# Sixteen consecutive tokens per partition, and V kept on chip with a shifted copy

## The chip, the cores and the metric

The kernel runs on one core of a Trainium2 chip. The metric is the device time of one execution in microseconds; lower is better. The core's engines work side by side, each through its own list of instructions in a fixed order: TensorE (PE, with PEld for its weight loads), VectorE (DVE), ScalarE (ACT), GpSimd (POOL) and SyncE (SP), which here only issues DMAs. DMAs are also issued from ACT and POOL. Sixteen DMA engines carry them all.

## The reference

2048 tokens of width 512 are normalised, and three terms are added: the input, a sliding dilated attention, and a gated MLP that mixes tokens.

```python
x = A_x                                   # (1, 2048, 512)
xn = layernorm(x)
# A: 32 heads of 16; each token looks at 8 tokens: itself and 2, 4, ... 14 before it
qkv = xn @ wqkv
idx = pos[:, None] - 2 * arange(8)[None, :]          # masked where negative
logits = einsum('bhsd,bhswd->bhsw', q, k[idx]) * 16 ** -0.5
o = einsum('bhsw,bhswd->bhsd', softmax(logits), v[idx])
A = o.reshape(B, S, D) @ wo
# B: gated MLP, hidden width 2 * 896
z = gelu(xn @ w_in)
z1 = z[..., :896]
z2 = layernorm(z[..., 896:])
g = einsum('ts,bsf->btf', w_sp, z2) + b_sp[None, :, None]     # w_sp is 2048 x 2048
B_ = einsum('bsf,fd->bsd', z1 * g, w_out)
return x + A + B_
```

## The kernel before

All tensors on chip lie in one bf16 array, `arena`, in which regions are reused as they fall free; fp32 scalars lie in `fpool`. Python code adds tasks (`T`, `dma`) with what they read and write; a planner derives the waits from these and from overlaps of the ranges, and the order of each engine's tasks is written out by hand in `plan.orders`, one list for each of PE, ACT, DVE, POOL and SP. An engine works through its list strictly in that order. Two tasks whose ranges overlap, one of them writing, are ordered as the program adds them.

Tokens come in 16 blocks of 128, in four groups j of 512. The first part of the program runs group by group:

- `ln_block(b)`: statistics of a block of x on DVE (L647, L650), the inverse root on POOL (L652), the normalisation on DVE (L662), then a transpose into `xnT`, on PE for the first four blocks and by DMA (L666) for the others.
- `qk_pair(j, c)`: Q and K of a group (L733), with heads interleaved so that four chunks c hold them, and one eviction by ACT for both (L741). The last 16 columns of K are copied by POOL into the next group's pad (L747). Q and K have two buffers each, by j % 2.
- `v_block(b)`: V of 128 tokens (L713), evicted by ACT (L717) and written to a scratch tensor in DRAM, `vscr`, by POOL's DMAs (L720).
- `prod_reduce(j)`: DVE multiplies Q with eight shifted views of K, 128x4096 (`prod`, L757). Of the four chunks' products some are summed on DVE (`psum`, L762), chosen by `npadd`, and PE sums over the dimensions and what is left (`stream`, L772, tasks `lg`). ACT evicts the logits (L794) and a DMA transposes them (L798, tasks `pT`).
- `softmax(j)`: on DVE and ACT for each group when its logits are there (L809 to L846; the exp at L826).
- `z2_block`, `z2_sq`, `z2_wave(j)`: the second half of the MLP's input with GELU (L856, L862), its squares (L913), mean and variance for four blocks (L921 to L931), the inverse root on POOL (L934) and the normalisation on DVE (L937), then sums of blocks T1 to T4 for the gate (L954).
- `z1_block(b)`: the first half (L900, L907).

The second part runs over eight tiles t, each of two times 128 tokens. `ld_w` transposes the rows of `w_sp` of a tile by two DMAs (L963, tasks `w`, two slots by t % 2); `s_sums` adds blocks of them on DVE (L975 to L981); `gate_parts` makes the gate by seven products of eight matmuls each (L1017, tasks P1 to P7), a Strassen-like scheme in which ACT copies partial results (L1032, L1035) and DVE finishes (L1059, L1063); `u_op` multiplies by z1 on DVE (L1041) and transposes by DMA (L1043, `uT`). `pv_pair` reloads nine shifted rows of V for 128 partitions from `vscr` (L1144, 1152 KB a pair), multiplies by the attention weights (L1152), sums (L1156, L1160) and transposes by DMA (L1165, `OTd`). `out_block` loads the residual (L1184), puts it into PSUM by ACT (L1191), adds the two output products (L1196 with `wo`, L1200 with `w_out`), evicts (L1209) and stores (L1212). `w_out` is loaded at L1128 and `wo` at L1131, whose DRAM side is `[[512, 4], [16*512, 32], [4*512, 4], [1, 512]]`.

In this program a partition holds every fourth token of 512: `tok(b)` gives the first token and the step 4 for z1, the gate, V and the output.

Of the kernel before, what the change touches and what calls it, by code (L numbers as in the profile page):

```python
# [14 lines left out]
class Plan:  # L15
# [288 lines left out]
BF = mybir.dt.bfloat16  # L304
F16 = mybir.dt.float16
F32 = mybir.dt.float32
ALU = mybir.AluOpType
# [11 lines left out]
    npadd=((1, 2), (1, 2, 3), (1, 2, 3), (1, 2, 3)),  # L319
# [5 lines left out]
def build_kernel(nc, A_x, A_wqkv, A_wo, B_x, B_w_in, B_w_sp, B_b_sp, B_w_out, out, report=False, sched_kw=None,  # L325
# [17 lines left out]
    VR = 8 + S // 2  # L343
    vscr = nc.dram_tensor("vscr", (2 * VR, 512), BF).ap()

    def tok(b):
        return (512 * (b // 4) + b % 4, 4)

    def rows(ap2, b):
        t0, ts = tok(b)  # L350
        w = ap2.shape[1]
        return bass.AP(tensor=ap2.tensor, offset=ap2.offset + t0 * w, ap=[[ts * w, 128], [1, w]])
# [3 lines left out]
    NT = 8  # L356
    off = {}
    base = 0
    for k, v in dict(xin=0, xn=2048, wqk=4096, wv_raw=8192, xin2=10240, Vn=12288).items():
        off[k] = base + v  # L360
    off["W"] = base
    base += 16384
    off["OT"] = base
    off["xnT"] = base
    base += 4 * S
    off["w_in"] = base
    off["w_out"] = base
    off["wo"] = base + FC * 512
    base += 7168
    off["QT"] = base  # L370
    off["KT"] = base + 4 * 512 * NQ
    ksz = 2 * 4 * (512 + KP)
    off["Vs"] = off["QT"]
    base = off["KT"] + ksz
    off["pb"] = base
    off["L"] = base + 8192
    off["Ve"] = base + 9728
    off["On"] = base + 4608
    off["yout"] = base + 6656
    off["xres"] = base + 8192  # L380
    veo = (0, -9728)
    base += 14336
# [8 lines left out]
    off["maskt"] = base + FH  # L391
# [3 lines left out]
    off["zeros"] = base  # L395
    off["Za"] = base
    base += 512
    for name, n in (("R", 128), ("ident", 128), ("mx", 128), ("Zb", 256), ("hm", 32), ("bsb", 16)):
        off[name] = base
        base += n  # L400
        base = (base + 15) & ~15
# [4 lines left out]
    for name, n in (("prime", 4), ("Z", 128), ("st6", NB * 9),  # L406
                    ("mv", NB * 2), ("vpe", NB), ("rstd", NB), ("s1", 2 * NB), ("s2", NB), ("m2", NB), ("msq", NB),
                    ("vpe2", NB), ("rstd2", NB), ("mhalf", 4), ("bias", NB), ("P5s", 2 * HF)):
        foff[name] = fb
        fb += n  # L410
# [4 lines left out]
    with ExitStack() as es:  # L415
# [36 lines left out]
        def k_off(c, j):  # L452
            return off["KT"] + (4 * (j % 2) + c) * (512 + KP) + KP

        for c in range(4):
            for j in range(NJ):
                R(("KTpad", c, j), "sb", [(k_off(c, j) - KP, k_off(c, j))])
                R(("QT", c, j), "sb", [(q_off(c, j), q_off(c, j) + 512)])
                R(("KT", c, j), "sb", [(k_off(c, j), k_off(c, j) + 512)])
        for s_ in range(NPB):  # L460
            R1(("pb", s_), "pb", 4096, 4096 * s_)
        for s_ in range(2):
            R1(("On", s_), "On", 1024, 1024 * s_)
            R1(("Vs", s_), "Vs", 4096, 4096 * s_)
            R1(("Ve", s_), "Ve", 4608, veo[s_])
            for r_ in range(2):
                R1(("w", s_, r_), "W", 2048, 8192 * s_ + 2048 * r_)
                R1(("g", s_, r_, 0), "g", HF, FH * (2 * s_ + r_))
                R1(("g", s_, r_, 1), "g", HF, FH * (2 * s_ + r_) + HF)
            for r_ in range(4):  # L470
                R1(("S", s_, r_), "W", 1024, 8192 * s_ + 4096 + 1024 * r_)
            R(("P5s", s_), "f", [(foff["P5s"] + HF * s_, foff["P5s"] + HF * s_ + HF)])
        for s_ in range(4):
# [3 lines left out]
            R1(("Vn", s_), "Vn", 512, 512 * s_)  # L477
        for s_ in range(3):
            R1(("xres", s_), "xres", 512, 512 * s_)
            for q in range(8):  # L480
                R1(("yout", s_, q), "yout", 64, 512 * s_ + 64 * q)
# [14 lines left out]
        for b in range(NB):  # L496
            R(("xnT", b), "sb", [(off["xnT"] + dc * S + 128 * b, off["xnT"] + dc * S + 128 * b + 128)
                                 for dc in range(4)])
            R1(("OT", b), "OT", 512, 512 * b)
# [6 lines left out]
        for nm, lo, hi, h0, h1 in (("w_in1", 0, FH, 0, 4), (("w_in2a", 0), FH, FH + HF, 0, 2),  # L506
                                   (("w_in2a", 1), FH, FH + HF, 2, 4), (("w_in2b", 0), FH + HF, 2 * FH, 0, 2),
                                   (("w_in2b", 1), FH + HF, 2 * FH, 2, 4)):
            R(nm, "sb", [(off["w_in"] + dc * 1792 + lo, off["w_in"] + dc * 1792 + hi) for dc in range(h0, h1)])
# [7 lines left out]
        R1("maskt", "maskt", 1024)  # L517
        R1("L", "L", 1024)
# [15 lines left out]
        def dma(eng, fn, nbytes, chan, reads=(), writes=(), name="", xbar=False, prio=None, lat=1700.0):  # L534
# [6 lines left out]
        maskt = ar[0:4, off["maskt"]: off["maskt"] + 1024]  # L541
# [17 lines left out]
        T("pool", lambda g: g.memset(AC(off["KT"], [[512 + KP, 4], [1, KP]]), 0.0),  # L559
          writes=[("KTpad", c, 0) for c in range(4)], est=200, name="ktpad", prio=2)  # L560
        def setup_masks():
# [8 lines left out]
            mv = maskt.rearrange("p (q w h) -> p q w h", q=4, w=8)  # L570
            T("pool", lambda g: g.affine_select(out=mv, in_=mv, pattern=[[1, 4], [-2, 8], [0, 32]], compare_op=ALU.is_ge,
                                                fill=NEG_BIG, base=0, channel_multiplier=4),
              writes=["maskt"], est=900, name="mask1", prio=2)
# [9 lines left out]
        def ld_win(nm, lo, n, eng, after=()):  # L583
            dma(eng, lambda e: e.dma_start(AC(off["w_in"] + lo, [[1792, 4], [1, n]]),
                                           B_w_in[:, lo: lo + n].rearrange("(c p) n -> p c n", p=128)),
                512 * n * 2, nm, reads=after, writes=[nm], name="ld" + nm)

        def ld_win_h(nm, lo, n):
            for h in range(2):
                dma(("sp", "act")[h], (lambda h: lambda e: e.dma_start(  # L590
                    AC(off["w_in"] + lo + 2 * 1792 * h, [[1792, 2], [1, n]]),
                    B_w_in[256 * h: 256 * h + 256, lo: lo + n].rearrange("(c p) n -> p c n", p=128)))(h),
# [4 lines left out]
        ld_win_h("w_in2a", FH, HF)  # L597
        ld_win_h("w_in2b", FH + HF, HF)
# [107 lines left out]
        def v_block(b):  # L706
            k = next_bank()
            sl = b % 4

            def mm(t):  # L710
                last = None
                for dc in range(4):
                    last = t.matmul(bank(k), AC(off["xnT"] + dc * S + 128 * b, [[1, 128]]),  # L713
                                    AC(off["wv_raw"] + 512 * dc, [[1, 512]]), start=(dc == 0), stop=(dc == 3))
                return last
            T("pe", mm, reads=[("xnT", b), "wv_raw"], writes=[("ps", k)], est=4 * c_mm(512), name="V%d" % b)
            T("act", lambda a: a.activation(A("Vn", 512, 512 * sl).rearrange("p (d h) -> p d h", d=16),  # L717
                                            bank(k).rearrange("p (h d) -> p d h", d=16), ACTF.Copy),
              reads=[("ps", k)], writes=[("Vn", sl)], est=c_act(512), name="Ve%d" % b)
            dma("pool", lambda e: e.dma_start(  # L720
                bass.AP(tensor=vscr.tensor, offset=vscr.offset + (8 + 64 * b) * 512, ap=[[512, 64], [VR * 512, 2], [1, 512]]),
                A("Vn", 512, 512 * sl)),
                128 * 512 * 2, ("vwr", sl), reads=[("Vn", sl)], writes=[("vscr", b)], name="Vw%d" % b)

        def qk_pair(j, c):
# [20 lines left out]
            if j < NJ - 1:  # L746
                T("pool", lambda g: g.tensor_copy(AC(k_off(c, j + 1) - KP, [[1, KP]]), AC(ko + 512 - KP, [[1, KP]])),  # L747
                  reads=[("KT", c, j)], writes=[("KTpad", c, j + 1)], est=400, name="halo%d_%d" % (j, c))

        def prod_reduce(j):  # L750
            NPD = cfg["npadd"][j]

            def prod(c, s_):
# [4 lines left out]
                  reads=[("QT", c, j), ("KT", c, j), ("KTpad", c, j)], writes=[("pb", s_)],  # L758
# [23 lines left out]
            for c in range(4):  # L782
# [5 lines left out]
                else:  # L788
                    prod(c, s1)
                    if c < 3:  # L790
# [4 lines left out]
                AC(off["L"], [[256, 4], [128, 2], [1, 128]]),  # L795
                PC(512 * 6, [[1, 4], [512, 2], [4, 128]]), ACTF.Copy),
              reads=[("ps", 6), ("ps", 7)], writes=["L"], est=c_act(1024), name="lge%d" % j)
            dma("sp", lambda e: e.dma_start_transpose(AC(off["attn"] + 1024 * j, [[128, 8], [1, 128]]),  # L798
                                                      A("L", 1024)),
                128 * 1024 * 2, "pT", reads=["L"], writes=[("attn", j), ("pTd", j)], name="pT%d" % j, xbar=True)  # L800

        def softmax(j):
            d0 = 1024 * j
            dk = ("attn", j)
            if j == 0:
                mv = ar[0:4, off["attn"]: off["attn"] + 1024]
                T("dve", lambda v: v.tensor_tensor(mv, mv, maskt, ALU.add), reads=["maskt"], writes=[dk],
                  est=c_dve(1024, 2.0), name="smask", prio=FILL)
# [12 lines left out]
            if j == 0:  # L821
                return
            js = (0, 1) if j == 1 else (j,)
            n = 1024 * len(js)
            ev = A("attn", n, 1024 * js[0])
            T("act", lambda a: a.activation(ev, ev, ACTF.Exp), writes=[("attn", i) for i in js],  # L826
              est=c_act(n, psum=False), name="sexp%d" % j, tbl="exp", prio=-1)
            for i in js:
                softmax_tail(i)
# [18 lines left out]
        def z2_block(b):  # L848
            if b >= 4:
                k = next_pair()  # L850

                def mm2(t):
                    last = None
                    for dc in range(4):
                        for hf in range(2):
                            last = t.matmul(ps[:, 512 * (k + hf): 512 * (k + hf) + HF], AC(off["xnT"] + dc * S + 128 * b, [[1, 128]]),  # L856
                                            AC(off["w_in"] + 1792 * dc + FH + HF * hf, [[1, HF]]),
# [10 lines left out]
            for hf in range(2):  # L868
                k = next_bank()
                c0 = FH + HF * hf  # L870
# [3 lines left out]
                def mm(t, hs, first, k=k, c0=c0):  # L874
                    last = None
                    for h in hs:
                        for dc in (2 * h, 2 * h + 1):
                            st = AC(off["attn"] + 512 + 128 * dc if b == 0 else off["xnT"] + dc * S + 128 * b, [[1, 128]])
                            last = t.matmul(ps[:, 512 * k: 512 * k + HF], st, AC(off["w_in"] + 1792 * dc + c0, [[1, HF]]),
# [473 lines left out]
```

## Time and profile before

| what | value |
|---|---|
| median of 3 runs | 237.26 us (237.12 to 238.02) |
| the profiled execution | 239.06 us, of it the span from first to last instruction 237.3 us |
| mean granted TensorE clock | 0.986 |
| busy | PE 225.0, DVE 213.8, ACT 124.7, POOL 61.6 us |
| DMA | 39.69 MB, 167 GB/s on average |
| products at L757 and L1152 | 16 each of 2.28 us on DVE |
| sums at L762 | 11 of 2.27 us on DVE |
| normalisations at L937 | 16 of 0.51 us on DVE |
| squares at L913 | 16 of 0.95 us on ACT |
| first gate product starts | 106.58 us |

The page shows, of one execution, how long each engine was busy, which work ended the waits of which, and the costliest groups of instructions. Lines such as L1017 are lines of the program; an arrow `ps<-arena` says what is written and read. A busy PE isn't PE at its peak, since matmuls are pipelined. The clock of TensorE that was granted is shown as a share of full speed, the DMA share as the busy part of the sixteen DMA engines. "issue" in a chain of waits is time in which an engine waited for nothing that the profile shows.

### The profile page before, as it was taken

How to read it: one execution, taken by the hardware profiler on the slowest of the kernel's cores; microseconds unless marked ns; L12 is line 12 of the kernel's file. 1: busy time of each engine (PE TensorE's matmuls, PEld its weight loads, DVE VectorE, ACT ScalarE, POOL GpSimd, SP SyncE). 2: the span in 40 equal slices, each digit the busy share in tenths (PEclk: the TensorE clock that was granted, in tenths of full speed). 3: DMA queues.
4: the chain of work that ended last, by engine and by line, in shares of the span. 5: the costliest groups of instructions: out<-in, count | busy, mean ns of one | idle time of the engine just before them, and what ended most of it. 6: DMA issues, size and time to landing. Idle time of an engine off the chain costs nothing.

```text
span 237.3 us, 3195 instructions
## 1 busy us (share of the span) xinstructions
PE 225.0 (95%) x1172; PEld 115.2 (49%) x1184; DVE 213.8 (90%) x262; ACT 124.7 (53%) x218; POOL 61.6 (26%) x64
## 2 busy tenths in 40 slices
PE   6999999998998899979999997999999999999995
PEld 5454454453453356544545543544545444454434
DVE  4759999999799989989999997999999999999920
ACT  4387776997688389594412451500534142342532
POOL 3325989999800650650000000000000000000000
PEclk9799999999999799999999999999999999999999
DMA  6896314752399401072699999999996999669761
GB/s 207 251 251 153 116 68 90 150 163 46 91 261 200 92 22 31 16 259 57 143 151 225 202 233 188 288 310 217 219 268 136 226 160 315 231 148 147 168 149 44
DMA packets 81668, 39.69 MB, mean 167 GB/s; under 512 B 69616, under 2 KB 80112, under 8 KB 80628
## 3 DMA queue, kind: packets, MB, share of 16 engines
q1 hardware_dynamic: 75540, 32.68, 64.2%
q10 hardware_dynamic: 5296, 4.69, 6.6%
q0 software_dynamic: 816, 2.12, 2.6%
q8 instruction: 9, 0.15, 0.3%
q14 instruction: 7, 0.06, 0.1%
HBM read 18.49 MB, written 4.21 MB: 96 GB/s over the span
## 4 chain that ended last, share of the span: by engine, by line
DVE 60%; issue 13%; POOL 10%; DMA 8%; PE 4%; POOLq 2%; SPq 1%; ACT 0%; ACTq 0%; DVEq 0%
DVE arena L1152 13%; DVE arena L1156 8%; DVE arena L757 7%; DVE arena L762 7%; POOL fpool L652 5%; DMA arena<-arena 4%; DVE arena L954 3%; DVE arena L975 3%; POOL fpool L934 3%; DMA arena<-in_A_x_dram 2%; DVE arena L1041 2%; POOLq L415 2%; DMA arena<-in_B_w_in_dram 2%; DVE arena L981 2%; DVE arena L979 2%
## 5 line engine op out<-in xcount | busy, mean ns | idle before, releaser
L1017 PE MATMUL ps<-arena 128*128 128x448 f16 (+1 forms) x448 | 87.4, 353 | 1.6 <-ACT arena L907 1.3
L1017 PEld LDWEIGHTS ps<-arena 128*128 128x128 f16 (+1 forms) x448 | 43.4, 98 | 44.2 <-ACT arena L907 1.7
L757 DVE TENSOR_TENSOR arena<-arena 128x4096 bf16<-128x4096 bf16 x16 | 36.3, 2278 | 0.0
L1152 DVE TENSOR_TENSOR arena<-arena 128x4096 bf16<-128x4096 bf16 x16 | 36.1, 2279 | 0.0
L1032 ACT ACTIVATE ps<-ps 128x448 f32<-128x448 f32 x16 | 8.4, 528 | 47.5 <-DVE arena L1059 23.7
L733 PE MATMUL ps<-arena 128*128 128x512 bf16 x126 | 28.3, 379 | 0.1
L1156 DVE TENSOR_TENSOR arena<-arena 128x4096 bf16<-128x4096 bf16 (+1 forms) x16 | 27.9, 1746 | 0.0
L1200 PE MATMUL ps<-arena 128*128 128x512 bf16 (+2 forms) x126 | 27.1, 355 | 0.0
L900 PE MATMUL ps<-arena 128*128 128x448 bf16 x128 | 26.3, 366 | 0.0
L762 DVE TENSOR_TENSOR arena<-arena 128x4096 bf16<-128x4096 bf16 x11 | 25.0, 2274 | 0.0
L733 PEld LDWEIGHTS ps<-arena 128*128 128x128 bf16 x128 | 14.5, 113 | 13.2
L652 POOL TENSOR_TENSOR fpool<-fpool 128x1 f32<-128x1 f32 x16 | 17.5, 1105 | 11.8 <-DVE fpool L650 11.8
L900 PEld LDWEIGHTS ps<-arena 128*128 128x128 bf16 x128 | 14.6, 116 | 11.0 <-issue 2.0
L856 PE MATMUL ps<-arena 128*128 128x448 bf16 x96 | 19.5, 357 | 0.0
L934 POOL TENSOR_TENSOR fpool<-fpool 128x4 f32<-128x4 f32 x4 | 12.4, 3096 | 25.7 <-DVE fpool L931 25.7
L741 ACT ACTIVATE arena<-ps 128x1024 bf16<-128x1024 f32 x16 | 16.1, 1025 | 4.3 <-PE ps L733 4.2
L907 ACT ACTIVATE arena<-ps 128x896 bf16<-128x896 f32 x16 | 14.6, 916 | 6.9 <-PE ps L900 6.7
L1196 PE MATMUL ps<-arena 128*128 128x512 bf16 (+2 forms) x65 | 15.4, 353 | 2.8 <-DMA arena<-arena 2.4
L1209 ACT ACTIVATE arena<-ps 128x512 bf16<-128x512 f32 (+2 forms) x17 | 9.3, 562 | 16.6 <-PE ps L1200 16.6
L1200 PEld LDWEIGHTS ps<-arena 128*128 128x128 bf16 x126 | 11.9, 98 | 12.4
L747 POOL COPY arena<-arena 128x16 bf16<-128x16 bf16 x12 | 15.8, 1330 | 2.1 <-ACT arena L741 2.1
L1035 ACT ACTIVATE arena<-ps,fpool 128x448 bf16<-128x448 f32 x16 | 10.0, 630 | 11.3 <-PE ps L1017 10.9
(86 smaller groups left out, 265.5 us busy)
## 6 DMA issues: line engine op xcount, KB each, us to landing
arena<-vscr SPq DMA_DIRECT2D x8, 1152.0 KB, 6.6
arena<-in_A_x_dram ACTq DMA_DIRECT2D x17, 128.0 KB, 3.1
vscr<-arena POOLq DMA_DIRECT2D x16, 128.0 KB, 2.5
arena<-in_A_x_dram SPq DMA_DIRECT2D x15, 128.0 KB, 3.0
out_dram<-arena ACTq DMA_DIRECT2D x15, 128.0 KB, 2.7
arena<-in_A_wqkv_dram SPq DMA_DIRECT2D x3, 512.0 KB, 5.7
arena<-in_B_w_in_dram SPq DMA_DIRECT2D x1, 896.0 KB, 5.1
arena<-in_B_w_out_dram SPq DMA_DIRECT2D x1, 896.0 KB, 13.3
```

The costliest lines, as they stand in the source:

```text
L652: T("pool", lambda g: g.tensor_tensor(Fv("rstd", 1, b), Fv("mv", 1, 2 * b + 1), Fv("mhalf", 1), ALU.pow), reads=[("mv", b), "mhalf"], writ ...
L733: last = t.matmul(bank(k + which), AC(off["wqk"] + 1024 * dc + col0, [[4, 128]]), AC(off["xnT"] + dc * S + 512 * j, [[1, 512]]), start=(dc ...
L741: T("act", lambda a: a.activation(AC(qo, [[ko - qo, 2], [1, 512]]), ps[:, 512 * k: 512 * k + 1024].rearrange("p (t n) -> p t n", t=2), ACT ...
L757: T("dve", lambda v: v.tensor_tensor(pbv, qb, kb, ALU.mult), reads=[("QT", c, j), ("KT", c, j), ("KTpad", c, j)], writes=[("pb", s_)], est ...
L762: T("dve", lambda v: v.tensor_tensor(A("pb", 4096, 4096 * a), A("pb", 4096, 4096 * a), A("pb", 4096, 4096 * b), ALU.add), reads=[("pb", b) ...
L856: last = t.matmul(ps[:, 512 * (k + hf): 512 * (k + hf) + HF], AC(off["xnT"] + dc * S + 128 * b, [[1, 128]]), AC(off["w_in"] + 1792 * dc + ...
L900: lastm = t.matmul(ps[:, 512 * (k + hf): 512 * (k + hf) + HF], AC(off["xnT"] + dc * S + t0, [[ts, 128]]), AC(off["w_in"] + 1792 * dc + HF ...
L934: T("pool", lambda g: g.tensor_tensor(Fv("rstd2", 4, 4 * j), Fv("vpe2", 4, 4 * j), mhalf, ALU.pow), reads=[("vpe2", j), "mhalf"], writes=[ ...
L1017: last = t_.matmul(pb_(k_), st(k), mv(k), start=(start and k == 0), stop=(k == 7), skip_group_check=True)
L1152: T("dve", (lambda iv, tv, av: lambda v: v.tensor_tensor(tv, iv, av, ALU.mult))(iv, tv, av), reads=[("attn", j), ("Ve", so)], writes=[("Vs ...
L1156: T("dve", (lambda n: lambda v: v.tensor_tensor(AC(off["Vs"], [[4096, 2], [1, n]]), AC(off["Vs"], [[4096, 2], [1, n]]), AC(off["Vs"] + n, ...
L1200: last = t.matmul(po, AC(off["z1"] + FH * tb + 128 * fc, [[1, 128]]), AC(off["w_out"] + 512 * fc + c0, [[1, n]]), start=False, stop=(fc == ...
```

## The change

A partition now holds 16 consecutive tokens (partition p: tokens 16 p to 16 p + 15), in place of every fourth of 512. Block b is the tokens 16 p + b. So the 14 tokens behind a token lie mostly in its own partition.

- z1 and V read `xnT` with a step of 16 columns, so they need all of `xnT`; V moves behind z1 in the program and in PE's list.
- V stays in `arena`, 16 slots of 512. One DMA on SP's queue, `Vhalo`, copies slots 2 to 15 of partitions 0 to 126 to the 14 slots ahead of V in partitions 1 to 127; another, `Vzero`, fills those of partition 0. `vscr`, its writes and its reloads are gone, and a product at `pv_pair` reads eight slots with a step of two.
- Logits of all four groups are written into one region `L` in the new order and transposed after all are made; the softmax of a group then runs with an exp of its own. The mask is added to 32 columns before the transpose.
- `npadd` has one DVE sum less for each group; PE adds these products instead (`stream` over two).
- K's two buffers lie side by side, so that most pads are not needed; the one left is copied by ACT (`halo`).
- The normalisation of z2 is done by ACT (`znact`), for which DVE makes `nb2`, minus mean times inverse root.
- The gate's tiles run from block 14 and 15 down to 0 and 1. Slot 1 of `w` lies over `xnT`.
- Residual loads and stores are made for two blocks together, 256 KB each, but for the last tile's stores.
- The five lists in `plan.orders` are new.

```diff
-    npadd=((1, 2), (1, 2, 3), (1, 2, 3), (1, 2, 3)),
+    znact=(1, 1, 1, 1),
+    npadd=((1,), (1, 2), (1, 2), (1, 2)),
...
+    off["W0"] = base
...
     off["xnT"] = base
+    woff = (off["W0"], off["xnT"])
...
+        R1("Vh", "V", 14 * 512, -14 * 512)
+        R("Vz", "sb", [(off["V"] - 14 * 512, off["V"])])
...
-        def v_block(b):
+        def v_block(q):
...
-                    last = t.matmul(bank(k), AC(off["xnT"] + dc * S + 128 * b, [[1, 128]]),
+                    last = t.matmul(bank(k), AC(off["xnT"] + dc * S + q, [[NTOK, 128]]),
...
-            dma("pool", lambda e: e.dma_start(
-                bass.AP(tensor=vscr.tensor, offset=vscr.offset + (8 + 64 * b) * 512, ap=[[512, 64], [VR * 512, 2], [1, 512]]),
-                A("Vn", 512, 512 * sl)),
...
-            if j < NJ - 1:
-                T("pool", lambda g: g.tensor_copy(AC(k_off(c, j + 1) - KP, [[1, KP]]), AC(ko + 512 - KP, [[1, KP]])),
+            if j == 1:
+                T("act", lambda a: a.activation(AC(k_off(c, 2) - KP, [[1, KP]]), AC(ko + 512 - KP, [[1, KP]]), ACTF.Copy),
...
-                        lastm = t.matmul(ps[:, 512 * (k + hf): 512 * (k + hf) + HF], AC(off["xnT"] + dc * S + t0, [[ts, 128]]),
+                        lastm = t.matmul(ps[:, 512 * (k + hf): 512 * (k + hf) + HF], AC(off["xnT"] + dc * S + b, [[NTOK, 128]]),
...
             for b in bl:
+                if cfg["znact"][j]:
+                    T("act", (lambda b: lambda a: a.activation(A("z2", FH, FH * b), A("z2", FH, FH * b), ACTF.Identity,
+                                                               bias=Fv("nb2", 1, b), scale=Fv("rstd2", 1, b)))(b),
...
+        for b in zord:
+            v_block(b)
+        ld_w(1)
+        for g_ in (3, 2, 1, 0):
+            logits_T(g_)
+        dma("sp", lambda e: e.dma_start(ar[1:128, off["V"] - 14 * 512: off["V"]], ar[0:127, off["V"] + 1024: off["V"] + 8192]),
+            127 * 14 * 1024, "Vh", reads=[("V", q) for q in range(2, NB)], writes=["Vh"], name="Vhalo")
+        dma("sp", lambda e: e.dma_start(bass.AP(tensor=ar, offset=off["V"] - 14 * 512, ap=[[AR, 1], [512, 14], [1, 512]]),
+                                        ar[0:14, off["zeros"]: off["zeros"] + 512]),
+            14 * 1024, "Vz", reads=["zeros"], writes=["Vz"], name="Vzero")
...
-            dma("sp", lambda e: e.dma_start(AC(vo, [[1, 9 * 512]]), src),
-                128 * 4608 * 2, ("Ve", so), reads=[("vscr", i) for i in range(4 * j - 1, 4 * j + 4)],
...
+                  reads=[("attn", q // 4)] + [("V", i_) for i_ in range(q % 2, q + 1, 2)] + (["Vh", "Vz"] if q < 14 else []),
```

The middle of PE's list, of DVE's list and of SP's list in the new program (P1_2 is product P1 of tile 2, u15 the product with z1 of block 15):

```
PE   ... z1_3 V12 V13 ... V3 V0 V2 P1_0 P5_0 bits P6_0 P2_0 P7_0 P3_0 P1_1 P4_0 P5_1 P6_1 P2_1 P7_1 P3_1
     P1_2 P4_1 P2_2 P5_2 P6_2 out14_0 P7_2 P3_2 P1_3 out15_0 ...
DVE  ... u14 ssub1 pva1024_0 g22_1 pvc0 sattn2 g12_1 S13_2 u12 S2_2 sz1_1 pv12 pv13 sz2_1 S4_2 ...
SP   ... w0_1 ldw_in1 pT3 pT1 ldwout pT2 pT0 w1_0 w1_1 Vhalo w2_0 w2_1 Vzero ldwo uT14 OTd0 w3_1 w3_0 uT15 w4_0 ...
```

## The prediction

> **What bounds the kernel now.** I read the page's busy shares first, then three stretches of the span, then what TensorE (PE) waited for, then the DMA rows.
>
> ```profile
> span 237.3 us, 3195 instructions
> ...
> PE 225.0 (95%) x1172; PEld 115.2 (49%) x1184; DVE 213.8 (90%) x262; ACT 124.7 (53%) x218; POOL 61.6 (26%) x64
> ```
>
> ```profile
> 15.43:106.58 91.15, 86.93 (x443) 44.30 (x447) 86.04 (x105) 70.50 (x114) 56.76 (x47) 0.98 0.49 117
> 106.58:237.30 130.72, 125.16 (x648) 62.73 (x655) 119.47 (x134) 45.72 (x82) 0.00 (x0) 1.00 0.90 192
> 128.85:237.30 108.45, 103.24 (x536) 51.91 (x541) 97.20 (x102) 37.55 (x69) 0.00 (x0) 1.00 0.93 204
> ```
>
> ```profile
> PE ps L772 <- DVE arena L762: 2.8, 2, 2.0
> PE ps L1196 <- DMA arena<-arena: 2.4, 2, 1.8
> PE ps L1017 <- ACT arena L907: 1.3, 1, 1.3
> ```
>
> The columns of the stretches are length, busy PE, PEld, DVE, ACT, POOL, granted clock, DMA share, GB/s. The first runs from the first Q/K matmul (15.43) to the first gate matmul, P1_0 (106.58), the second from there to the end. PE is 95% busy in both; VectorE (DVE) is close behind, and ScalarE (ACT) has room. The chain of waits runs through DVE for 60%, but PE itself stood still for only 6.5 us behind others after 15.43: 2.8 for logits that DVE had not summed, 1.3 before P1_0, 2.4 for late transposes. No change that leaves PE's work alone can gain much more than that.
>
> The DMA rows matter most for this change: the queues between 111 and 128 us (40 slices of 0.425 us) and the slices of the first 12 us.
>
> ```profile
> DMA  0002622222376999999999999992338223799969
> GB/s 0 0 0 82 205 75 80 89 65 82 82 101 130 299 279 198 176 149 198 198 154 166 205 177 144 235 143 94 103 106 99 99 86 57 161 290 290 202 146 215
> ...
> arena<-in_B_w_out_dram SPq DMA_DIRECT2D x1, 896.0 KB, 13.3
> arena<-in_A_wo_dram SPq DMA_DIRECT2D x1, 512.0 KB
> ```
>
> ```profile
> GB/s 0 0 0 0 0 0 133 236 307 191 204 287 356 370 308 308 358 370 371 376 386 371 244 54 14 34 133 321 253 266 123 55 222 311 362 379 382 382 382 375
> ```
>
> The load of wo (L1131) is issued at 111.68 and has the queues nearly to itself from 113.1 to 115.2: a share of 0.2 to 0.3 of sixteen engines, at 78 GB/s (mean of 75, 80, 89, 65, 82). Its DRAM side has 4 as its outermost count; so it runs on about four engines, some 20 GB/s each. The loads of the first 12 us, all 128 rows outermost, reach 382 GB/s: 24 GB/s an engine if sixteen were busy all the time, 26.5 at the 0.9 that the digit 9 stands for. And wo's four engines hold up what comes after it: w_out, 896 KB, lands after 13.3 us, where w_in's 896 KB took 5.1 on the page.
>
> **The change part by part, without the shifted copy.** DVE loses 4 of 11 sums at L762 (4 x 2.27 = 9.1 us), the 16 normalisations at L937 (16 x 0.51 = 8.1) and most of the mask's add (0.67), and gains 4 products of 128x4 (0.15 each, as L926). PE gets the 32 logits matmuls that replace these sums: 8 took 0.55 in the timeline (57.40 to 57.95), so 2.2. POOL loses 16 V writes (0.64 each) and 12 halo copies; little waited for it (3.5 at L937, 2.1 at L662). The queues lose the V writes and eight reloads of 1152 KB; the residual loads and output stores are paired, 256 KB with 2 KB rows.
>
> PE then reaches the end of the last V matmul at 106.58 - 0.78 - 1.97 - 1.25 (its three waits, gone if nothing replaces them) + 1.54 (z1_11, which stood behind P1_0) + 2.2 = 106.3. Is ACT in time? From z1_14 to that point its new list, by the spacing of such rows back to back, is 16 GELUs x 0.81, 16 V evictions x 0.48, 15 normalisations, 4 squares x 0.93, 2 z2 GELUs x 0.90, 3 evictions x 0.92, an exp with its table load 2.3, another exp 1.1. The normalisation (896 elements, SBUF to SBUF, two per-partition operands) has no row. L913's square starts its successor after 0.84; pointer operands add 0.1 (L1035's 0.63 against L1032's 0.53); I take 0.94, with 0.84 and 1.15 as ends. Sum 46.7. PE over the same list: 16 z1 x 1.52 + 2 z2 x 1.56 + 0.9 + 1.6 + 16 V x 0.865 = 43.7. So ACT, not PE, sets this stretch, by some 3 us less what the buffers absorb: I put the eviction Ve2, one of the last, at 109 (107 to 114). The halo copies, now 4 on ACT (0.2 each), hide there. DVE's T differences wait for the moved normalisations at about 92, an idle stretch that DVE can afford (97.2 busy in the last 108.45 before).
>
> z1 and V now load weights 16 elements apart. L900's, 4 apart, take 116 ns against 98 for adjacent ones; even 190 would lie under the 190 ns of a matmul (16.74 us for 88). I take nothing; 0 to 4 us (192 loads x 20 ns) if it sticks out.
>
> **The shifted copy.** Vhalo moves 127 partitions x 14,336 B = 1.82 MB inside SBUF. No copy of the trace has 127 rows. The ends are sixteen engines (382 GB/s, 4.8 us) and one. wo with its outermost 4 was dealt to four engines, so a copy seems to be dealt in equal parts; 127 is prime, and no number from 2 to 16 divides it. I take one engine. At 24 to 26.5 GB/s that is 76 to 69 us (91 at wo's 20, which are 1 KB rows; V's are far longer); I take 71.4.
>
> [...]
>
> When does it start? In SP's order: w1_0, w1_1, Vhalo, w2_0, w2_1, Vzero, ldwo, uT14, OTd0, ... w1 now lies over xnT and waits for the last V matmul, 106.5; two issues of 2.3 (median of L963) put w1_1's at 108.8; it lands 5.0 later (their median), and the shared engine turns to Vhalo at about 113. 113 + 71.4 = 184.4, landing 185.4.
>
> Who waits? On that engine, the sixteenth parts of w2_0 and w2_1, queued behind: w2_0 lands about 187, and P1_2 needs it. On DVE, S13_2 (w2), and behind it pv12 and pv13 (Vh, Vz) and all else. On SP, Vzero: its range overlaps the copy's, so it waits for the landing, and behind it stand ldwo, every uT and OTd, w3. So PE stops after P3_1, about 126, and resumes with P1_2 at 187. PE has then stood for 61 us: the row of 5 to 10 us (granted clock 0.71) lost 1.5 us so; I add that. From P1_2 on the work is the same as before: 108.45 from 128.85 (P1_2's start, between P3_1 and the rest of the 56 matmuls from 127.32) to the end. Its 2.4 us of DMA waits I keep: out14 now waits for wo, issued only after the landing (512 KB at 78 GB/s, 6.7 us, against the 7.7 of five products ahead of it on PE) and uT14 behind it.
>
> [...]
>
> Sum: 187 + 1.5 + 108.45 = 297.0 of span. The profiled execution of before took 237.3 of span (239.06 around it); the runs' median is 237.26, so span and median agree. **Forecast 297.**
>
> **Rivals.**
> - The copy is dealt over sixteen engines (faster). It then lands before 120, and S13_2 and pv12 want it at about 130 (S13_2 ran at 130.25). Time: 237.3 - 4.0 - 2.4 + 2.2 = 233.1. For it: every 128-row copy here does so; against: wo did not. 11%.
> - One engine, but w2 gets past it. PE goes on to out14, which waits for wo: 185.4 + 6.7 + 2 = 194, and from out0_0 before (138.18) 99.1 remain: 293. 7%.
> - One engine at wo's 20 GB/s: 113 + 91 + 2.6 + 110 = 317. 4%.
> - The copy is hidden, but ACT becomes the bound: 1.15 for a normalisation adds 16 x 0.21 = 3.4 to the 3, and DVE's T work, held until then, pushes the end: 240. It decides once a normalisation costs over 1 us. 4%.
>
> The forecast itself has 74%, with 284 to 314 as its own range: start 107 to 118, 69 to 80 us of copy, 106 to 110 of rest. That is also my range for all cases; it leaves out the first and last rivals and most of the third. Half a per cent, 1.2 us, is about what a measurement here tells from none: faster 12%, same 1%, slower 87%.
>
> **What would show it.** A stretch of some 60 us from about 126 with PE, DVE and ACT idle, a DMA share near 0.06, and then P1_2; a wait of SP at the Vzero issue of about 70 us; LDWEIGHTS of z1 and V below 190 ns; a normalisation of 1.0 us or less; logits waits gone. A share near 1 for 5 us after 113 and no gap would make me wrong at once; a gap of half the length would mean two engines' worth of speed.

## The result and the profile after

The changed kernel takes 294.85 us (median of 4 runs, 294.74 to 295.25) against 237.64 us for the kernel before beside it (4 runs, 237.12 to 238.29): a ratio of 1.241, 95% interval 1.237 to 1.245. It is 57.2 us slower; forecast were 297.0, with 284 to 314 as the range. The profiled execution after took 294.92 us, 293.2 of it span. Of the runs further down, one of norm_on_dve's six (237.87 us) was a slow one; its ratio leaves that run out, its median does not.

First the page of the changed kernel: span, busy shares, and the slices (40 of 7.33 us).

```profile
span 293.2 us, 3188 instructions
...
PE 226.4 (77%) x1202; PEld 122.1 (42%) x1216; DVE 198.0 (68%) x246; ACT 137.0 (47%) x237; POOL 32.3 (11%) x35
...
PE   8999999999999999900000000978999999999996
...
PEclk9999999999999999975555555799999999999999
DMA  7954627000016352000900004999679579553542
GB/s 228 275 125 109 129 54 197 0 2 0 0 36 171 97 122 45 25 27 27 45 25 27 27 27 95 124 207 180 147 183 183 139 156 175 128 134 91 152 98 72
```

PE's busy time hardly moved (225.0 before, 226.4 now); its share fell because a hole of eight slices opened in the middle. In the hole the queues move 25 to 27 GB/s at a digit of 0, which is one engine's worth (26.3 in the table below); the one slice with 45 GB/s and a 9 is a burst of w2, of which more below. The next view, busy time by stretches (length, PE, PEld, DVE, ACT, POOL, granted clock, DMA share, GB/s), says the same of the engines.

```profile
130.00:185.00 55.00, 1.89 (x6) 0.78 (x7) 0.00 (x0) 0.00 (x0) 0.00 (x0) 0.50 1.04 44
185.00:293.00 108.00, 102.89 (x531) 51.75 (x536) 93.58 (x94) 35.09 (x67) 0.00 (x0) 0.99 0.73 144
```

One column misleads here: this view gives a DMA share of 1.04 to a stretch in which next to nothing moves, because a packet that has been started and then stands counts as busy (twenty of w2's stood 38.9 to 39.4 us each, by the packet records, which makes 0.89 of the 1.04). The GB/s column is the one to trust (its 44 holds what moved after 180 us as well). After the hole PE is 95% busy, as before the change.

Who ended the hole? The waits (engine, line, what released it; total, times, longest), then the timelines of PE and of SyncE's queue (start, length, instructions, idle time before and its releaser):

```profile
DVE arena L971 <- DMA arena<-in_B_w_sp_dram: 61.2, 2, 58.1
PE ps L1012 <- DMA arena<-in_B_w_sp_dram: 59.2, 2, 58.4
...
DVE arena L951 <- ACT arena L930: 11.9, 2, 10.8
```

```profile
107.88 16.87 PE L1012 MATMUL ps<-arena 128*128 128x448 f16 x88
183.11 9.44 PE L1012 MATMUL ps<-arena 128*128 128x448 bf16 x40 [58.36 <-DMA arena<-in_B_w_sp_dram]
194.37 0.81 PE L1201 MATMUL ps<-arena 128*128 128x512 bf16 x3 [1.82 <-ACT fpool L1027]
```

```profile
104.62 4.32 SPq L959 DMA_TRANSPOSE arena<-in_B_w_sp_dram  x2
108.98 0.81 SPq L1118 DMA_DIRECT2D arena<-arena  x1
111.15 71.66 SPq L959 DMA_TRANSPOSE arena<-in_B_w_sp_dram  x2
182.86 0.86 SPq L1120 DMA_DIRECT2D arena<-arena  x1
183.76 0.65 SPq L1128 DMA_DIRECT2D arena<-in_A_wo_dram  x1
```

PE and DVE wait for the load of w_sp (w2), not for Vhalo: the copy harms first through what lies behind it in the queue. The forty matmuls take 9.44 us where 128 of the same pitch take 24.66 in wo_in_four below (7.71 for forty): the clock, granted at 0.81 over these 9.44 us, costs 1.7. SyncE issues Vhalo in 0.81 us at 108.98, and then needs 71.66 us to issue the two transposes of w2, 69.24 of it for the first.

The trace also records each DMA packet. Vhalo's are the only ones of 14,336 B, so they can be picked out; from these records, for the runs below as well:

```
kernel        pieces    engines   one row, median us (5 to 95%)   first row to last   GB/s
after         127          1      0.535 (0.535 to 0.544)          69.35 us             26.3
copy_on_act   127          1      0.535 (0.535 to 0.542)          71.32 us             25.5
split124      124 + 3    4 + 3    0.795 (0.535 to 1.067)          25.34 us             71.8
split126      126 + 1   14 + 16   0.535 (0.535 to 0.721)           5.41 us            334
split112      112 + 15  16 + 15   0.821 (0.579 to 1.078)           7.14 us            255
```

The records name the queue and not the engine, but the engine counts can be read off in two ways, and both agree with the table. The rows under way at once are one in after and copy_on_act (in after row follows row every 0.532 us, each lasting 0.535), four for 23.2 of split124's 25.34 us, fourteen for 4.6 of split126's 5.41, sixteen for 5.0 of split112's 7.14. And the trace records every raise of a copy's semaphore. As the pieces land there are 1 in after and copy_on_act, 4 and 3 in split124, 14 and 16 in split126, 16 and 15 in split112, besides one soon after the issue wherever there are fewer than sixteen. The single row of split126 is not in its row of the table: it went as sixteen packets of 896 B.

The records also show where w2 was. Of its 4,096 packets of 256 B only 503 started while Vhalo's rows ran, all between 140.4 and 141.6 us, and the next at 180.12, when the last row had ended. So nearly the whole of w2 stood, not only a sixteenth of it. Vhalo's semaphore was full at 180.60, that of w2_0 at 182.98, and PE resumed at 183.11.

### The profile page after: what moved, and what is told of

The parts are those of the page before. It is cut to its first block, busy times and chain, and to the rows that moved or that the text cites. A ratio compares the mean times of both kernels' runs of the same rounds, so it can differ in the third digit from the quotient of the medians.

```text
span 293.2 us, 3188 instructions
## 1 busy us (share of the span) xinstructions
PE 226.4 (77%) x1202; PEld 122.1 (42%) x1216; DVE 198.0 (68%) x246; ACT 137.0 (47%) x237; POOL 32.3 (11%) x35
## 4 chain that ended last, share of the span: by engine, by line
PE 42%; another core or an unknown queue 20%; ACT 18%; DVE 9%; DMA 5%; issue 3%; SPq 1%; POOL 1%; ACTq 0%; DVEq 0%
PE ps L1012 28%; PE ps L1205 8%; ACT arena L930 6%; ACT arena L898 4%; PE ps L1201 4%; DVE arena L754 4%; DMA arena<-in_B_w_sp_dram 2%; ACT arena L718 2%; DMA arena<-in_A_x_dram 2%; DVE fpool L647 2%; ACT arena L904 2%; ACT arena L855 2%; DVE arena L759 2%; DMA arena<-in_B_w_in_dram 1%
## 5 line engine op out<-in xcount | busy, mean ns | idle before, releaser
L1012 PE MATMUL ps<-arena 128*128 128x448 f16 (+1 forms) x448 | 89.0, 357 | 59.4 <-DMA arena<-in_B_w_sp_dram 59.2
L1012 PEld LDWEIGHTS ps<-arena 128*128 128x128 f16 (+1 forms) x448 | 43.9, 99 | 103.0 <-issue 62.0
L971 DVE TENSOR_TENSOR arena<-arena 128x2048 f16<-128x2048 bf16 x8 | 9.7, 1215 | 61.2 <-DMA arena<-in_B_w_sp_dram 61.2
L754 DVE TENSOR_TENSOR arena<-arena 128x4096 bf16<-128x4096 bf16 x16 | 36.3, 2280 | 4.2 <-PE ps L769 4.2
L1139 DVE TENSOR_TENSOR arena<-arena 128x4096 bf16<-128x4096 bf16 x16 | 36.3, 2281 | 0.0
L892 PE MATMUL ps<-arena 128*128 128x448 bf16 x128 | 25.2, 354 | 0.2 <-ACT arena L898 0.2
L652 POOL TENSOR_TENSOR fpool<-fpool 128x1 f32<-128x1 f32 x16 | 21.0, 1321 | 15.1 <-DVE fpool L650 15.1
L892 PEld LDWEIGHTS ps<-arena 128*128 128x128 bf16 x128 | 18.2, 145 | 7.0 <-ACT arena L898 0.6
L730 PEld LDWEIGHTS ps<-arena 128*128 128x128 bf16 x128 | 14.2, 113 | 14.4 <-issue 1.5
L849 PE MATMUL ps<-arena 128*128 128x448 bf16 x96 | 19.7, 353 | 0.0
L930 ACT ACTIVATE arena<-arena,fpool 128x896 bf16<-128x896 bf16 x16 | 18.9, 1207 | 0.0
L951 DVE TENSOR_TENSOR arena<-arena 128x896 f16<-128x896 bf16 (+1 forms) x16 | 9.5, 618 | 11.9 <-ACT arena L930 11.9
L1205 PEld LDWEIGHTS ps<-arena 128*128 128x128 bf16 x126 | 11.9, 98 | 12.4
L759 DVE TENSOR_TENSOR arena<-arena 128x4096 bf16<-128x4096 bf16 x7 | 16.0, 2288 | 0.1
L904 ACT ACTIVATE arena<-arena 128x896 bf16<-128x896 bf16 x16 | 15.3, 958 | 0.1
```

The costliest lines, as they stand in the source:

```text
L652: T("pool", lambda g: g.tensor_tensor(Fv("rstd", 1, b), Fv("mv", 1, 2 * b + 1), Fv("mhalf", 1), ALU.pow), reads=[("mv", b), "mhalf"], writ ...
L730: last = t.matmul(bank(k + which), AC(off["wqk"] + 1024 * dc + col0, [[4, 128]]), AC(off["xnT"] + dc * S + 512 * j, [[1, 512]]), start=(dc ...
L754: T("dve", lambda v: v.tensor_tensor(pbv, qb, kb, ALU.mult), reads=[("QT", c, j), ("KT", c, j), ("KT", c, j - 1) if j % 2 else ("KTpad", c ...
L759: T("dve", lambda v: v.tensor_tensor(A("pb", 4096, 4096 * a), A("pb", 4096, 4096 * a), A("pb", 4096, 4096 * b), ALU.add), reads=[("pb", b) ...
L892: lastm = t.matmul(ps[:, 512 * (k + hf): 512 * (k + hf) + HF], AC(off["xnT"] + dc * S + b, [[NTOK, 128]]), AC(off["w_in1"] + FH * dc + HF ...
L904: T("act", lambda a: a.activation(A("sqj", FH), A("z2", FH, FH * b), ACTF.Square, accum_out=Fv("s2", 1, b)), reads=[("z2h", b, 0), ("z2h", ...
```

## The experiments

All ratios are to the kernel before, run beside each on the same chip. The line numbers of a kernel with edits can be up to five off those of the changed kernel.

**split112: the same bytes, dealt over sixteen engines.** Two copies, of 112 and 15 partitions, in place of one of 127.

```diff
-ar[1:128, ...] <- ar[0:127, ...]                        # Vhalo
+for p0, p1 in ((0, 112), (112, 127)):
+    ar[p0 + 1:p1 + 1, ...] <- ar[p0:p1, ...]            # Vhalo0, Vhalo1
```

> The copy of 127 partitions is made as two, 112 and 15; same bytes, same shift, same place in the queue. My theory (a copy is dealt in equal parts to as many of the 16 engines as divide its outermost count): 112 rows go to 16 engines, 1.6 MB at 16 x 26 GB/s is 4 us, 15 rows go to 15 engines, under 1 us; both land before 118, the gap of 58 us on PE goes, time 233 to 237. Rival (a copy inside SBUF to the neighbouring partition is slow in itself, some 26 GB/s): still 290 or more.

Measured: 235.9 us (235.37 to 237.16, 6 runs) against 238.26, ratio 0.991 (0.988 to 0.994). The hole is gone, and the change with this one edit is a little faster than the kernel before (0.9%, with an interval below 1): the whole loss sat in how one DMA was dealt. The copy took 7.14 us and not the 5 expected, since its rows took 0.821 us. PE's timeline still shows two stops, and SyncE's queue shows what stood there:

```profile
136.30 0.81 PE L1204 MATMUL ps<-arena 128*128 128x512 bf16 x3 [1.74 <-DMA arena<-arena]
...
142.80 1.67 PE L1012 MATMUL ps<-arena 128*128 128x448 bf16 x8 [1.15 <-DMA arena<-in_B_w_sp_dram]
```

```profile
113.67 10.86 SPq L959 DMA_TRANSPOSE arena<-in_B_w_sp_dram  x2
...
125.44 0.65 SPq L1131 DMA_DIRECT2D arena<-in_A_wo_dram  x1
126.13 4.22 SPq L1038 DMA_TRANSPOSE arena<-arena  x1
130.46 3.29 SPq L1154 DMA_TRANSPOSE arena<-arena  x1
133.79 6.68 SPq L959 DMA_TRANSPOSE arena<-in_B_w_sp_dram  x2
```

**split124: four engines.** The same edit at 124 + 3.

> The copy is made as 124 and 3 partitions. My theory: 124 is 4 x 31, so 4 engines take 31 rows of 14336 B each, 445 KB at 26.5 GB/s, 16.8 us instead of 68; it ends about 128, w2_0 lands 129 to 130 and PE waits about 5 us: 237 to 242. Rival (uneven counts are simply rounded up over sixteen engines, and only a prime count goes to one): 233 to 237. Rival (slow in itself): 290 or more.

Measured, in one run: 252.57 us. PE's timeline and the DMA rows from 100 to 200 us (40 slices of 2.5 us):

```profile
140.40 10.07 PE L1012 MATMUL ps<-arena 128*128 128x448 bf16 x40 [15.64 <-DMA arena<-in_B_w_sp_dram]
```

```profile
DMA  2059939222322228992499789991949697926968
GB/s 84 21 127 210 112 91 100 57 69 69 92 69 75 80 56 188 186 107 90 107 193 283 161 191 193 209 208 39 270 99 186 120 213 196 210 70 144 193 137 172
```

From 117.5 us to the copy's end the digit is 2, once 3 (0.2 to 0.3 of sixteen), which is four engines, as expected, and four rows were under way at once; the time is not as expected, since four engines moved 71.8 GB/s and not 106. The packet records say how: some rows took 0.54 us, as alone, others 1.07, twice that. What they share was not tried.

**split126: a count of 14, against a power of two.**

> Edit: the copy as 126 + 1 partitions. Theory (the number of engines is the largest divisor of the outermost count that is at most 16: 14 for 126, 9 rows each): TensorE's gap between the last P3 of pair 1 and the first P1 of pair 2 stays under 2 us, 235 to 238. Rival (the number of engines is the largest power of two that divides the count: 2 for 126, 63 rows each at 0.535 us = 34 us): a gap of some 24 us, 258 to 264.

Measured, in one run: 232.86 us, below the 235 to 238 expected; the gap is as expected. The P1 of pair 2 starts as soon as P3_1 is through, and out14 waits for nothing:

```profile
128.45 4.71 PE L1012 MATMUL ps<-arena 128*128 128x448 bf16 x24 [0.19 <-ACT ps L1027]
133.22 0.81 PE L1204 MATMUL ps<-arena 128*128 128x512 bf16 x3
```

At 5.41 us, 126 rows of 0.535 need at least 12.5 engines on average, so the rival's two engines are out, and the largest divisor up to 16 fits all four large counts tried (127, 126, 124, 112) and the small pieces of 15 and 3 rows.

**vzero_free: is it SyncE standing at Vzero?** Vzero's range was taken out of the bookkeeping that makes it wait for the copy; the bytes it writes are others than the copy's.

```diff
-R("Vz", "sb", [(off["V"] - 14 * 512, off["V"])])
+R("Vz", "sb0", [(off["V"] - 14 * 512, off["V"])])
```

> The copy stays at 127 partitions; only the wait of Vzero for it is gone (their partitions differ), so that SP isn't held at Vzero and issues wo, uT14, OTd0 and w3 while the copy runs. My theory (the one engine is the bound, and every later transfer of SP's queue has a part on it behind the copy): the gap stays, PE resumes at the same 183, and only what came late after it is saved, 1.8 + 0.8 us of PE waits: 291 to 294. Rival (SP's standing at Vzero holds the kernel up): 250 or less.

Measured: 295.5 us, ratio 1.241 (1.237 to 1.245): no gain, not even the few us that my theory expected. SyncE's queue in that run:

```profile
111.76 71.92 SPq L959 DMA_TRANSPOSE arena<-in_B_w_sp_dram  x2
183.73 0.87 SPq L1120 DMA_DIRECT2D arena<-arena  x1
```

SyncE never reaches Vzero before the copy is through: it is still in the issue of w2. In after, too, Vzero was issued at 182.86, right behind w2, so there was no wait of its own to save.

**copy_on_act: another queue, w2 ahead in SyncE's.** Vhalo goes to ScalarE's queue, behind Ve0, and Vzero is free as above.

```diff
-dma("sp", ... name="Vhalo")
+dma("act", ... name="Vhalo")
```

> The copy of 127 partitions is issued from ACT's queue after Ve0, and Vzero doesn't wait for it. My theory: the copy still takes 68 us on one engine, 112 to 181, but w2_0 and w2_1 stand in SP's queue and get past it by turns; PE goes on until it needs S4_2, which stands on DVE behind pv12 and pv13, the first to read the copy. DVE stops at pv12 at about 131 instead of 127 and goes on at 182: 284 to 290. Rival (the engine takes transfers in order of issue, whatever queue): as before, 293 to 296.

Measured, in one run: 295.3 us, in the rival's range. My theory missed: w2 still waits for the whole copy, which starts at about the same time. SyncE's queue, and the DMA queues from 100 to 190 us (packets, MB, time of the packets as a share of sixteen engines):

```profile
104.96 77.86 SPq L959 DMA_TRANSPOSE arena<-in_B_w_sp_dram  x4
```

```profile
q1 hardware_dynamic: 9093, 2.57, 112.8%
q10 hardware_dynamic: 272, 2.08, 5.8%
```

q10 carries the copy, q1 the transposes. q1's packets fill more than sixteen engines' time with 2.57 MB, so they stand. The packet records show them in step with the copy: 223 to 241 packets of 256 B start in each 8 us, 16 to each 0.55 us, which is one for every engine per row of the copy if they are dealt evenly; w2_0 has 2,048 such packets, 128 an engine, and the copy has 127 rows. I read this as the two queues taking turns, one packet against one row, with the transpose advancing on all sixteen engines at the pace of the one that is shared. It is a reading of the equal counts; it was not varied. From SyncE's own queue, in after, w2 did not advance even so: there were the 503 packets and no more.

**wo_in_four: the two stops left in split112.** wo is loaded in four DMAs of 32 partitions each, in place of one whose outermost count is 4. Vzero is free of its wait besides, as in vzero_free; that changes nothing here, since in split112 Vzero was issued at 124.58, right behind w2 (113.67 + 10.86).

```diff
-AC(off["wo"], ...) <- ap=[[512, 4], [16 * 512, 32], [4 * 512, 4], [1, 512]]
+for a_ in range(4):
+    ar[32 * a_: 32 * a_ + 32, ...] <- offset + 512 * a_, ap=[[16 * 512, 32], [4 * 512, 4], [1, 512]]
```

> Edit: the copy in two pieces (112 + 15 partitions) as in split112; besides, the load of wo (512 KB), outermost dimension 4, becomes four loads of 32 partitions each (outermost 32), and the zeros no longer wait for the copy. In split112 TensorE still stands 1.74 us at 136.30 for SyncE's transposes and 1.15 us at 142.80 for w3, and wo's load is issued right ahead of them. Theory (a load whose outermost count is 4 occupies 4 of the 16 engines, and the transposes behind it wait for those four): both waits shrink to under 0.3 us, the three more issues on SyncE cost about 2 us of its queue, hidden; median 233.0 to 234.6, ratio to before 0.978 to 0.985. Rival (the two waits come from the length of SyncE's own issues): the waits stay or grow by the 2 us of issuing; 235.5 to 238.

Measured: 233.08 us (6 runs), ratio 0.980 (0.976 to 0.983). By the packet records wo went in 2.97 us, from 6.67 in split112. PE's timeline:

```profile
133.86 0.81 PE L1206 MATMUL ps<-arena 128*128 128x512 bf16 x3
...
140.25 1.68 PE L1013 MATMUL ps<-arena 128*128 128x448 bf16 x8 [1.04 <-DMA arena<-in_B_w_sp_dram]
```

The first stop is gone, the second is nearly what it was: the theory holds for the first only. In split126, with wo in one load, both were gone too; there the issue of w2 took 8.55 us in place of 10.86, and all behind it came earlier.

**norm_on_dve, split126_wo4 and split126_wo4_norm: does ScalarE set the stretch from z1 to the last V?** The 16 normalisations go back to VectorE, first on split112, then on split126 with wo in four.

```diff
-znact=(1, 1, 1, 1),
+znact=(0, 0, 0, 0),
```

> Edit: split112 with the 16 normalisations of z2 on VectorE again (each group of four just ahead of the first difference that reads it), so ScalarE has 16 x 1.03 = 16.5 us less and VectorE 16 x 0.51 = 8.1 us more. The prediction's step (ScalarE's list, 46.7 us from z1 of token 14 to the last V, sets that stretch against TensorE's 43.7): the last V ends up to 3 us earlier, median 232.5 to 234.5, ratio 0.975 to 0.985. Rival 1 (TensorE, busy 47.1 of the 48 us from 58 to 106 in split112, is the bound there too): 235 to 236.5, ratio 0.986 to 0.994, the same as split112. Rival 2 (the normalisations hold VectorE's softmax and differences and TensorE waits for these): 237 or more, ratio 0.995 or more.

> Edit: the copy as 126 + 1 partitions, wo in four loads of 32 partitions, the zeros free of the copy. The one look at split126 had none of the two waits that split112 (1.74 + 1.15 us) and wo_in_four (1.04 us) still had, at 232.9 us. Theory (with both edits no DMA holds TensorE after the start): 232.0 to 233.5, ratio 0.974 to 0.982. Rival (split126 alone was a lucky single run, and the two edits add up): below 231.5.

> Edit: split126_wo4 with the 16 normalisations on VectorE again, as in norm_on_dve. What norm_on_dve left open, told apart on the same chip. If ScalarE sets the stretch from z1 to the last V: 0.9 to 1.5 us below split126_wo4 (TensorE's idle time between 58 and 106 was 0.84 us with ScalarE, 0.20 us with VectorE), 231 to 232.3. If TensorE sets it: within 0.5 us of split126_wo4. If VectorE becomes the bound: above it.

Measured: norm_on_dve 235.01 us, ratio 0.987 (0.983 to 0.991), against split112's 0.991, which lies in the range of its Rival 1 and settles nothing by itself; split126_wo4 233.37 us, ratio 0.981 (0.977 to 0.985); split126_wo4_norm 231.79 us, ratio 0.974 (0.969 to 0.979). Both pairs point the same way, by 1 to 1.6 us, and in both the intervals overlap. The stretch itself is clearer. From 58 to 106 us, split126_wo4 and then split126_wo4_norm (columns as above):

```profile
58.00:106.00 48.00, 47.16 (x255) 30.81 (x256) 32.05 (x45) 47.95 (x66) 2.02 (x2) 1.00 0.18 47
```

```profile
58.00:106.00 48.00, 47.89 (x263) 32.02 (x264) 41.08 (x66) 35.63 (x52) 2.24 (x2) 1.00 0.21 54
```

With the normalisations ScalarE works 47.95 of 48 us; without them 35.63, and PE does eight matmuls more. PE is nearly full in both (47.16 and 47.89), so little more can be had there. P1_0 starts at 104.4 to 106.3 in after, split112, split124, split126, wo_in_four and split126_wo4, which normalise on ScalarE, and at 103.4 and 102.9 in the two that do it on VectorE. The one run of split126 alone (232.86) and five runs of split126_wo4 (233.37) show no gain of the second edit on top of the first.

**before_wo4: is the gain of wo the change's?** The kernel before with that edit alone.

> Edit: the kernel before with wo in four loads and nothing else: how much of the gain of wo_in_four has nothing to do with the change. There wo is issued at 111.7, 4.5 us ahead of the transposes of w2 and 30 us ahead of the first matmul that reads it, so theory: the same, ratio 0.995 to 1.003. Rival: w2's transposes start sooner and the wait of 1.77 us at 145.3 goes, ratio 0.988 to 0.994.

Measured: 238.45 us against 238.42, ratio 1.000 (0.997 to 1.003). There wo is issued ahead of w2 and is out of the way in time; the edit pays only where the change has put wo behind w2 and ahead of the transposes that PE needs next. The version to keep is split126_wo4_norm: 231.79 us.

## Why the prediction was right, step by step

- **One engine.** Right, and the heart of it. 127 rows at 0.535 us one after the other are 67.9 us; from first to last 69.35 against 71.4 forecast. The same bytes over sixteen engines left no hole. In the trace one row is under way at a time, 14,336 B in 0.535 us, which is 26.8 GB/s. Ahead of the result the traces showed only wo for it (an outermost 4, a share of 0.2 to 0.3); for 127 rows the step was an inference.
- **Its start.** Some 2 us early. The issue of w1 began at 104.62, where the end of the last V at 106.5 was to release it; Vhalo was issued right behind it at 108.98, and its first row started at 110.77, where the engine was to turn to it at about 113.
- **The resumption.** 187 forecast, 183.11 measured; this holds the whole miss, 3.9 us (297.0 was forecast as span, which came to 293.2). 2.2 of it is the start and 2.05 the copy's length, less 0.4 for what follows the last row (2.6 forecast, 2.99 measured).
- **Who waits for w2, and why.** Right that w2 comes in behind the copy and that PE and DVE wait for it; the way was another. The prediction put a sixteenth of w2 behind the copy on the shared engine; in the trace nearly all of w2 stood (503 of 4,096 packets), and SyncE was held in the issue of w2_0 until 180.39. Both bring w2 in just behind the copy. Why the issue is held is open.
- **Span and time.** Some luck: the forecast is a span, put for a time because the span before, 237.3, happened to be the runs' median. After, the span of 293.2 and the time of 294.92 are 1.7 apart, so the median was missed by 2.1 and the span by 3.8.
- **The clock.** 1.5 forecast; forty matmuls in 9.44 against 7.71 make 1.7. The granted clock was 0.50 in the hole (130 to 183) and from 183.11 to 186.00, 0.92 to 190.00 and 1.00 from there, 0.81 over the 9.44 us, which alone would make 1.8.
- **The rest.** 108.45 and 1.5 forecast, 293.2 - 183.11 = 110.1 measured; out14 did wait, 1.82 us.
- **SyncE at Vzero.** Wrong in its place: SyncE stood 71.66 us in the issue of w2, one step earlier. It cost nothing, since w2 held PE and DVE to the same moment; vzero_free, without Vzero's wait, was no faster.
- **DVE held at S13_2** by w2: right (58.1 us). Its T differences waited 10.8 us for the normalisations, as expected, in a stretch that could afford it.
- **The normalisation on ScalarE.** I took 0.94 us with 0.84 and 1.15 as ends; back to back the next instruction comes 1.03 later (each recorded 1.2 us long):

```profile
65.90 1.15 ACT L930 ACTIVATE arena<-arena,fpool 128x896 bf16<-128x896 bf16 x1
66.93 0.93 ACT L855 ACTIVATE arena<-ps 128x896 bf16<-128x896 f32 x1
...
104.82 2.08 ACT L718 ACTIVATE arena<-ps 128x512 bf16<-128x512 f32 x4
```

```profile
L892 PEld LDWEIGHTS ps<-arena 128*128 128x128 bf16 x128 | 18.2, 145 | 7.0 <-ACT arena L898 0.6
...
L930 ACT ACTIVATE arena<-arena,fpool 128x896 bf16<-128x896 bf16 x16 | 18.9, 1207 | 0.0
```

- **ScalarE's list.** Its terms as they stand add up to 46.4 and not 46.7; measured are 46.25, from z1 of block 14 at 60.65 to the end of Ve2 at 106.90 (the last line of ScalarE's above). So the size was right, the normalisations' excess being made up by other rows; Ve2 at 109 (107 to 114) was not, as the list began earlier. ScalarE is indeed the fuller engine there (47.95 of 48), but the 240 us of the fourth rival did not come: with the copy out of the way and 1.03 a piece, split112 took 235.9. Its threshold of 1 us was too low.
- **The wide stride of the weights.** Right that it costs nothing: 145 ns a load (L892 and L714; 116 at L900 before), under the 190 of a matmul (16.87 us for 88), and L892's matmuls take 354 ns as modelled, like L1012's float16 ones.
- **The logits waits** of PE are gone, and nothing of their size took their place.
- **The rivals.** The sixteen engines' 233.1 was 2.8 below split112's 235.9, which still stood 1.74 and 1.15 us for late transposes; split126 took 232.86 in its one run. w2 did not get past the copy, even from another queue.

## What to carry to other kernels

Look at the outermost count of both sides of every large copy: here 127, a prime, put 1.82 MB on one engine (69.35 us), and cutting off one row (126 + 1) made it nearly 13 times as fast (5.41 us); wo, with 128 partitions on the chip and an outermost 4 in DRAM, took 6.67 us, and 2.97 as four loads of 32. The price of such a copy is more than its own landing: what was queued behind it came late first (PE waited 58.36 us for w2), so ask which loads come next, and do not count on another queue to get them past (here it did not: 295.3 us in copy_on_act). Getting w2 past the copy would not have been the cure either: pv12, the copy's own reader, stands four places behind S13_2 in VectorE's list, and with w2 past the copy I estimated (in copy_on_act) still 284 to 290 us; no run got there. When a change moves work onto an idle engine, measure the stretch where that engine is fullest: here ScalarE had room over the span (137.0 of 293.2 us busy) and none between 58 and 106 us (47.95 of 48).

## What the runs showed of the hardware that was not expected

- SyncE was held in the issue of a transfer for as long as the copy ran: the first of w2's two transposes took 69.24 us to issue, until 180.39, where the copy's last row ended at 180.12 and the median in the same kernel is 2.21.
- Transposes of 256 B packets seem to advance on sixteen engines in step: with one engine taken up by rows of 0.535 us, sixteen packets in all started per 0.55 us (copy_on_act).
- More engines did not always mean more speed: rows took a median of 0.535 us on one engine and at 14 (334 GB/s in all, split126), but 0.795 at 4 (72 GB/s) and 0.821 at 16 (255 GB/s), and 0.734 at 14 in split126_wo4_norm. So the number of engines alone does not set it. Why is open.
